# New order of the mixed section of polynomial attention and a gated feed-forward layer, with the last tokens' products written permuted

## The chip, the cores and the metric

The kernel runs on one core of a Trainium2 chip. Its engines are TensorE (PE, with its weight loads as PEld), VectorE (DVE), ScalarE (ACT), GpSimd (POOL) and SyncE (SP, which here only issues transfers). TensorE writes its results to PSUM; GpSimd does not read PSUM in this kernel. The metric is the device time of one launch in microseconds: 286.42 us before the change, the median of three runs (286.40 to 286.61).

## The reference

Attention with a polynomial feature map, then a feed-forward layer with a sigmoid gate, all in float32:

```python
def phi(x):                                   # q, k, v: (4, 4, 1088, 32); S1, S2: (8, 32)
    a = np.einsum('rd,bhsd->bhsr', S1, x)
    b = np.einsum('rd,bhsd->bhsr', S2, x)
    return np.einsum('bhsi,bhsj->bhsij', a, b).reshape(*x.shape[:-1], r * r)
kv = np.einsum('bhsf,bhsd->bhfd', phi(k), v)
z = np.sum(phi(k), axis=2)
attn = np.einsum('bhsf,bhfd->bhsd', phi(q), kv) / (np.einsum('bhsf,bhf->bhs', phi(q), z)[..., None] + 1e-06)
x = attn.transpose(0, 2, 1, 3).reshape(4352, 128)
gate = 1.0 / (1.0 + np.exp(-(x @ w_gate)))    # w_gate, w_val: (128, 1536)
out = (gate * (x @ w_val)) @ w_out            # w_out: (1536, 128)
```

## The kernel before

The 4352 tokens of x lie transposed in SBUF (xT, 128 features by tokens) and are cut into nine chunks: eight of 512 tokens and a last one of 256. The first five chunks are computed in "waves" (w1, line 690), mixed with the attention of the four batches. When the attention is done, at about 177 us, `section()` computes the last four chunks: three of 512 tokens and the last 256.

Within a chunk, the 32 tokens of a partition block are 34 tokens apart in the output, since the attention's tiles take every 34th token of a batch.

**How the section computes gate and value.** For 128 columns of w_gate and the same 128 of w_val, the two products with a chunk form a 2 by 2 problem: gate and value on one side, the two halves of the 128 features between, and two halves of the chunk's tokens on the other. Seven products of half size do the work of eight, with sums of weights (fw) and of tokens (yt) made before. They are P1 to P7 in `feature_of` (line 1561). Each takes 64 rows (the lower or the upper half of the array), 128 columns of weights in two halves of 64, and 256 tokens. One wave w holds two such sets of 128 columns: P1 to P7 for the first, P1' to P7' for the second. Waves 0 to 17 are the three chunks of 512 tokens (six waves each). Waves 18 to 21 are the last 256 tokens; there an entry issues four matmuls over 128 tokens, and the six pairs of column sets are dealt as `ends = ((0, 2), (1, 3), (4,), (5,))`, so that waves 20 and 21 have no primed products.

A wave uses three PSUM banks, A, V and C, and passes through these entries (`gated`, line 1612; ACT entries begin with A or S, DVE entries with D or M):

| entry | engine | what it does | it needs |
|---|---|---|---|
| P1, P2 | PE | add to A | P2 after Aa |
| Aa | ACT | V = A (L1623) | P1 and P1' |
| P6, P7, P4 | PE | add to V | P6 and P7 after Aa; P7 after D1 has read V; P4 after D2 has read V |
| P5, P3 | PE | add to C | P3 after D1 |
| Ac | ACT | s5 = C (L1625) | P5 and P5' |
| D1 | DVE | C = V + s5 (L630) | P6, P6', Ac |
| D2 | DVE | c2 = V + s5 (L630) | P7, P7' |
| Sa, Sc | ACT | sigmoid of A, of C (L1627) | P2; P3 |
| M1, M2 | DVE | g = V times Sa; g = c2 times Sc (L1633, L1635) | P4, Sa; D2, Sc |

A bank is taken again by a later wave once its readers are done. The number behind "=" in an entry names the bank or buffer that it takes.

**The product with w_out** is done in the same way. Q0 to Q3 (`token_sum`, line 1637, POOL) make sums of g over tokens. WLA, WUA, WLB, WUB and WFA, WFB (`w_out`, line 1588) add to two accumulators A and B: L and U name the half of the rows, F all 128 rows at once; the number is the pair of column sets, and -2 and -1 are the two that the waves left over. EA and EB (`empty`, line 1650) copy an accumulator out with ACT and move halves of it across partitions by DMA; chunk numbers go from -1 (the waves' last) to 2. F0 to F6 (`total`, line 1669) add the parts with DVE, transpose (L1683), and store with four or eight transfers on SP (`store`, L550). T0 to T3 (`x_sum`) are POOL's sums of tokens for a chunk.

**The last 256 tokens** end differently (`last`, line 1686). Their g is the stationary operand, in 64 tokens by 128 rows, and w_out's rows stream past it, so the result has tokens on its partitions. O0 and O1 add to the first of two banks (`end`), O2 and O3 to the second. `store_end` (line 560) copies the first bank with ACT and the second with DVE into o_end and stores each with one transfer, the first from ACT's queue and the second from SP's (L566).

**What sets the order.** The four compute engines take their instructions in the order in which the program issues them, and the section issues them in the order of the string `ORDER` (lines 19 to 68): 740 entries, of which 444 are TensorE's. Each engine's order is that of its own entries in it; an engine waits when an operand or a bank is not free. Transfers are issued by SP's queue in the order of their calls, and by ACT's in EA:2, EB:2 and the end.

Of the kernel before, what the change touches and what calls it, by code (L numbers as in the profile page):

```python
# [16 lines left out]
P = 128  # L17

ORDER = """
P5:1=4 P1':0=5 P1:0 P1:1=0 P5':0=1 P1':1 Aa:0=2 WLA:-2.1 WUB:-2.0 Aa:1=3 P5':1 P5:0 P2':0 P6':0 Ac:1=0  # L20
P6':1 P6:0 Ac:0=1 WUB:-1.0 WLA:-1.0 D1:0 P2:1 P6:1 P2':1 P2:0 D1:1 P7':0 P3':0 Sa:0=0 P7:0 P3:0 Sa:1=1
P3':1 P7:1 D2:0=2 Sc:0=3 P1':3=5 P7':1 P5:2=0 P3:1 M2:0=0 P5':2 P4':0 Sc:1=4 D2:1=5 Q0:0 P4:0 P1:2=1
Ac:2=1 WUA:-2.0 P1':2 M1:0 WUB:-1.1 P4:1 Aa:2=4 M2:1=1 P4':1 P1:3 P6:2 P2':2 Aa:3=2 M1:1 Q0:1 P2:2 P6':2
P2':3 P6:3 T0:1 D1:2 P5:3=3 P6':3 T1:1 P5':3 WLB:-2.0 WLA:-1.1 Ac:3=0 Q1:1 P3':2 P2:3 D1:3 P7:2 P3:2 Q1:0
Sa:3=6 WLA:-2.0 P7':2 Sa:2=7 Q2:1 P7':3 P3':3 D2:2=8 Sc:2=2 P3:3 P5':4=5 P1':5=1 P7:3 M2:2=2 Sc:3=3 P4':2
P1':4=0 D2:3=0 P4:2 P1:4 WUA:-1.1 P5:4 Aa:4=3 M1:2 P4':3 P1:5 Ac:4=1 M2:3=3 P4:3 WUA:-1.0 Aa:5=4 WUA:-2.1
P2':4 M1:3 Q0:3 P6:4 P2:4 P6':4 P6:5 Q0:2 Sa:4=4 P5':5=2 WLB:-1.0 D1:4 Q2:0 P6':5 P5:5 P2:5 WLB:-1.1
Ac:5=0 Q1:3 P7:4 P3:4 EA:-1 D1:5 P7':4 P3':4 Q1:2 P1:6=0 P2':5 Sc:4=5 D2:4=1 Q2:2 P1':6 WUA:1.1 Sa:5=2
P3:5 P7:5 T2:1 Aa:6=5 P3':5 P7':5 EB:-1 Q3:2 P5:6=1 WUA:1.0 D2:5=8 P5':6 P4':4 T3:1 P6':6 WLB:1.1 Ac:6=1
Q3:1 P2:6 P4:4 Sc:5=7 P4:5 P6:6 Q3:0 WUA:0.1 P4':5 D1:6 P2':6 WUA:0.0 Q2:3 M1:4=4 WLB:3.1 P1:7=2 Sa:6=0  # L30
Q3:3 WLB:0.0 P1':7 M2:5=5 WUA:2.0 WLB:1.0 Aa:7=3 P5':7=0 WLB:3.0 M2:4 P6':7 P5:7 P3':6 P7:6 M1:5 Ac:7=0
Q0:4 P3:6 P7':6 P2':7 P6:7 Sc:6=3 Q1:4 D2:6=6 WUA:4.1 WLB:2.0 D1:7 Q2:4 P1':8=4 WUA:2.1 P5:8=1 P2:7 F0:-1
WUA:4.0 P1:8 Sa:7=4 F1:-1 P5':8 P3':7 F2:-1 Aa:8=2 P3:7 P7':7 M2:6=6 P7:7 P4':6 Sc:7=7 P2:8 WUB:0.0
D2:7=8 Ac:8=1 Q0:6 P4:6 WLA:3.1 F4:-1 WUB:3.1 WLA:0.1 P1':9=0 P4':7 F3:-1 P6:8 WLA:3.0 M1:6 WLA:0.0 P1:9
P4:7 WUB:1.1 Aa:9=5 Q0:5 WLA:1.0 WUB:2.0 M1:7=0 T0:2 P6':8 P6':9 P6:9 WUB:3.0 D1:8 Q3:4 WLA:2.0 P5':9=3
F5:-1 P5:9 WLA:2.1 Q1:6 WLA:1.1 P2':9 Ac:9=0 P7':8 P2':8 D1:9 Q2:6 P3:8 P7:8 Sa:8=1 WLA:4.0 P2:9 D2:8=5
T1:2 P7:9 WUB:1.0 F6:-1 P3:9 P3':8 Q1:5 P1':10=4 P3':9 Sc:8=2 Q2:5 P7':9 P4':8 Sa:9=3 P4:8 P1:10 Q3:5
D2:9=6 Sc:9=0 P5:10=1 WUB:4.0 Aa:10=0 M2:7 P5':10 WUB:5.1 P1:11=3 P4':9 Ac:10=1 M1:8=2 Q0:7 P2':10 P1':11
M2:8 P4:9 P6':10 Aa:11=2 Q1:7 P2:10 WUA:3.0 M1:9=1 P6:10 P6':11 Sa:10=4 WUA:3.1 WLB:5.1 D1:10 Q3:6
P5':11=5 P6:11 M2:9 WLB:5.0 P5:11 Q2:7 P1':12=4 WUA:5.1 Ac:11=0 P3:10 WUA:5.0 D1:11 P1:12 P7:10 Q0:9  # L40
# [12 lines left out]
WUB:8.0 WLA:10.1 M1:14 WLA:8.0 P6':16 T0:3 P4':15 P6:16 Q1:14 P2:16 P1:17=0 D1:16 WUB:11.1 WLA:9.0 Q0:13
M2:15=2 WLA:9.1 P5':17=3 T1:3 WUB:9.0 P3:16 P3':16 P7:16 M1:15 WLA:10.0 P1':17 Q2:14 Sc:16=6 WLA:11.0
P7':16 Aa:17=2 Q1:13 WLA:11.1 P5:17 D2:16=3 P2':16 WUB:10.0 Ac:17=0 Q2:13 M2:16=1 P2:17 P6:17 EA:1 Q3:12
P6':17 P2':17 Sa:16=7 P1:18=1 P4:16 D1:17 Sa:17=0 P4':16 P1':18 Q3:13 WUB:11.0 WLA:12.0 Aa:18=4 M1:16
P3:17 P5':18=0 EB:1 Q0:16 P6:18 WLA:13.0 F2:1 P6':18 P5:18 Q0:15 P2:18 P3':17 Ac:18=1 WUB:13.1 P7:17
Sc:17=1 D1:18 Q3:14 P7':17 P1:19=5 P1':19 P2':18 F0:1 Q1:15 P7:18 P3':18 Aa:19=3 D2:17=4 P3:18 P7':18
Sa:18=5 F1:1 P6:19 WUA:12.0 Q2:15 Sc:18=8 WUA:12.1 P4:17 D2:18=2 P2':19 P1:20=1 Q1:16 P5:19=0 P4':17
P5':19 WLB:13.0 M1:17=3 T3:3 P2:19 P6':19 Ac:19=0 Q2:16 P4:18 WLB:13.1 Sa:19=3 D1:19 P5:20=2 P4':18 Q3:15  # L60
Aa:20=5 WLB:12.0 WUA:13.1 M1:18=4 Ac:20=1 Q3:16 P7':19 P6:20 P3':19 P7:19 D1:20 P2:20 P3:19 D2:19=6 P7:20
WLA:12.1 Sa:20=7 F3:1 Sc:19=0 WUB:12.0 WLA:13.1 M2:18 P1:21=1 P4:19 P5:21=4 P4':19 F4:1 Aa:21=0 WUB:13.0
P3:20 M2:17 Ac:21=0 P6:21 WUA:13.0 F5:1 WFA:14.0 Q0:17 F6:1 WFA:14.1 D1:21 Q1:17 WFA:15.1 M1:19=6
WFB:16.0 Q2:17 M2:19 WFA:15.0 Q3:17 WFA:16.1 WFA:17.0 D2:20=5 WFA:17.1 WFA:16.0 WFB:17.0 EA:2 WFB:17.1
# [7 lines left out]
def kernel(  # L72
# [17 lines left out]
    NTOK, DM = out.shape  # L90
# [4 lines left out]
    T = S // 32  # L95
# [62 lines left out]
    T0 = 2 * q_chk[0][1]  # L158
# [112 lines left out]
    HALF = TCH // 2  # L271
# [288 lines left out]
    def store_end(acc):  # L560
        b, r = divmod(tok_chk[-1][0], S)
        o_sb = [sbA.tile([P, P], F32, tag="nd", name="o_end") for _ in range(2)]
        for u, copy in enumerate((nc.scalar.copy, nc.vector.tensor_copy)):
            copy(out=o_sb[u], in_=acc[u])
        for u, eng in enumerate((nc.scalar, nc.sync)):
            eng.dma_start(  # L566
                out=bass.AP(
                    tensor=out.tensor,
                    offset=out.offset + (b * S + r // 32 + u) * DM,
                    ap=[[2 * DM, 4], [T * DM, 32], [1, DM]],  # L570
                ),
                in_=o_sb[u],
            )
# [932 lines left out]
    def section():  # L1506
# [41 lines left out]
        def end_g(w):  # L1548
            return gs[home["g", w]].rearrange("p (q u t) -> p q u t", u=2, t=HALF // 2)
# [62 lines left out]
        def gated(k, w):  # L1612
            n = parts_of(w)
            at = lambda x: bank[home[x, w]][:, :n]
            s5, c2 = (lambda: s5s[home["s5", w]][:, :n]), (lambda: smalls[home["c2", w]][:, :n])
            if w < N:
                two = lambda x: x.rearrange("p (j t) -> p j t", j=2)
                g = lambda u: g_of(w)[:, :, u * HALF : (u + 1) * HALF]
            else:
                two = lambda x: x.rearrange("p (q t) -> p q t", t=HALF // 2)  # L1620
                g = lambda u: end_g(w)[:, : 2 * n // HALF, u]
            if k == "Aa":
                nc.scalar.copy(out=at("V"), in_=at("A"))  # L1623
            elif k == "Ac":
                nc.scalar.copy(out=s5(), in_=at("C"))  # L1625
            elif k in ("Sa", "Sc"):
                nc.scalar.activation(out=smalls[home[k, w]][:, :n], in_=at(k[1].upper()), func=ACTF.Sigmoid)  # L1627
            elif k == "D1":
                add(at("C"), at("V"), s5())
            elif k == "D2":  # L1630
                add(c2(), at("V"), s5())
            elif k == "M1":
                nc.vector.tensor_tensor(out=g(0), in0=two(at("V")), in1=two(smalls[home["Sa", w]][:, :n]), op=MUL)  # L1633
            else:
                nc.vector.tensor_tensor(out=g(1), in0=two(c2()), in1=two(smalls[home["Sc", w]][:, :n]), op=MUL)  # L1635
# [135 lines left out]
```

## Time and profile before

| | us |
|---|---|
| median of three runs | 286.42 |
| the profiled execution | 286.56 |
| its span | 284.5 |
| first product of the section | 177.03 |
| first copy of the section's last result (ACT, L564) | 279.66 |
| copies out of the accumulators (ACT, L1659), 128x512, one | 0.58 |
| V and C copies (ACT, L1623 and L1625), 128x512, one | 0.57 |
| sums and gated products (DVE, L630, L1633, L1635), 128x512 / 128x256, one | 0.69 / 0.42 |
| token sums (POOL, L528 and L1648), 128x256, one | 0.72 |

The span is what the profiler sees of the program; the execution's time is 2.06 us longer. "Busy" is the share of the span in which at least one instruction of an engine runs. TensorE runs at its full granted clock throughout (0.997 in the mean). Start times are read from the span's begin.

### The profile page before, as it was taken

To read this page: it belongs to the slowest core of one execution; us is meant where nothing else is said; L and a number is where in the kernel's file an instruction comes from. 1 tells how busy PE (TensorE), PEld (TensorE's weight loads), DVE (VectorE), ACT (ScalarE), POOL (GpSimd) and SP (SyncE) were. 2 spreads that over 40 slices of the span, in tenths; PEclk is the share of its full clock that TensorE was granted. 3 is DMA by queue.
4 is the path that set the end of the run, shared out by engine and by line. 5 is a ranking of instruction groups with operands and counts; after the bars stand their busy time and mean duration, and the time that the engine had idled before them with its cause. 6 is when DMAs were issued, how large, how long until landed. Compare 5 with 4: busy or idle time off the path is not lost.

```text
span 284.5 us, 8360 instructions
## 1 busy us (share of the span) xinstructions
PE 277.5 (98%) x3444; PEld 169.1 (59%) x3444; DVE 207.1 (73%) x349; ACT 123.2 (43%) x242; POOL 177.5 (62%) x238
## 2 busy tenths in 40 slices
PE   8899999999999999999999999999999999999993
PEld 4454433354444444544444544679889889999783
DVE  6987788946778777677769758576777766877861
ACT  3689833222335222533325223566536445465230
POOL 2666673567486578663978764367748784797400
PEclk9999999999999999999999999999999999999998
DMA  7995441674781376554368412100400130121133
GB/s 221 348 365 144 94 158 42 156 135 120 225 184 28 82 168 151 128 158 106 74 159 158 116 27 54 24 2 13 112 3 12 31 85 2 21 45 26 21 68 56
DMA packets 33630, 29.32 MB, mean 103 GB/s; under 512 B 19256, under 2 KB 28024, under 8 KB 33592
## 3 DMA queue, kind: packets, MB, share of 16 engines
q1 hardware_dynamic: 29188, 25.70, 36.5%
q10 hardware_dynamic: 4404, 3.08, 4.2%
q8 instruction: 27, 0.44, 0.7%
q14 instruction: 11, 0.09, 0.1%
HBM read 20.60 MB, written 3.26 MB: 84 GB/s over the span
## 4 chain that ended last, share of the span: by engine, by line
PE 97%; ACT 1%; POOL 0%; DVE 0%; issue 0%
PE wave L690 36%; PE b L538 25%; PE prod L538 23%; PE moeout L582 4%; PE warm L383 2%; PE kvz L1035 1%; PE nps L1393 1%; PE kps L816 1%; PE kvz L1022 1%; PE cqps L962 1%; PE nps L1225 0%; PE denj L1164 0%; PE nps L1177 0%; PE dps L1206 0%; ACT asb L933 0%; POOL gh L850 0%
## 5 line engine op out<-in xcount | busy, mean ns | idle before, releaser
L690 PE MATMUL wave<-xT,w_sb 128*64 128x512 f32 (+2 forms) x436 | 117.4, 589 | 0.1
L538 PE MATMUL prod<-tsum,ws 64*64 64x256 f32 (+1 forms) x348 | 85.7, 379 | 0.0
L538 PE MATMUL b<-yt,fw 64*64 64x256 f32 (+1 forms) x1056 | 77.8, 352 | 0.0
L698 ACT ACTIVATE sg<-wave 128x512 f32<-128x512 f32 x60 | 35.8, 597 | 89.8 <-PE wave L690 85.7
L690 PEld LDWEIGHTS wave<-xT,w_sb 128*64 128x64 f32 (+1 forms) x436 | 40.0, 143 | 46.2 <-issue 35.9
L528 POOL TENSOR_TENSOR tsum<-g,tsum 128x256 f32<-128x256 f32 x48 | 46.2, 963 | 30.3 <-DVE g L725 30.0
L725 DVE TENSOR_TENSOR g<-wave,sg 128x512 f32<-128x512 f32 x60 | 41.1, 685 | 27.3 <-ACT sg L698 26.5
L538 PEld LDWEIGHTS b<-yt,fw 64*64 64x64 f32 x1056 | 54.1, 133 | 7.3 <-issue 1.5
L538 PE MATMUL prod<-g,w_sb 64*64 64x256 f32 (+2 forms) x234 | 56.6, 377 | 0.0
L528 POOL TENSOR_TENSOR tsum<-g 128x256 f32<-128x256 f32 x48 | 41.6, 866 | 16.8 <-DVE g L725 16.5
L538 PEld LDWEIGHTS prod<-tsum,ws 64*64 64x64 f32 (+1 forms) x348 | 43.0, 135 | 9.4 <-issue 6.0
L1648 POOL TENSOR_TENSOR tsum<-g 128x256 f32<-128x256 f32 x36 | 26.9, 760 | 27.1 <-DVE g L1635 21.0
L538 PE MATMUL prod<-tsum,w_sb 64*64 64x256 f32 (+1 forms) x116 | 34.1, 380 | 0.0
L538 PEld LDWEIGHTS prod<-g,w_sb 64*64 64x64 f32 (+1 forms) x234 | 26.4, 135 | 12.6 <-issue 9.3
L538 PE MATMUL prod<-g,ws 64*64 64x256 f32 (+1 forms) x116 | 33.2, 378 | 0.0
L538 PE MATMUL b<-yt,w_sb 64*64 64x256 f32 (+1 forms) x288 | 30.8, 351 | 0.0
L1648 POOL TENSOR_TENSOR tsum<-g,tsum 128x256 f32<-128x256 f32 x36 | 26.9, 760 | 1.2
L1627 ACT ACTIVATE sg<-b 128x512 f32<-128x512 f32 (+1 forms) x34 | 18.9, 580 | 17.0 <-PE b L538 13.8
L630 DVE TENSOR_TENSOR b<-b,s 128x512 f32<-128x512 f32 (+1 forms) x22 | 14.7, 672 | 10.7 <-ACT s L1625 6.7
L538 PEld LDWEIGHTS b<-yt,w_sb 64*64 64x64 f32 x288 | 18.4, 133 | 1.7 <-ACT b L1623 0.2
L538 PEld LDWEIGHTS prod<-g,ws 64*64 64x64 f32 (+1 forms) x116 | 15.5, 135 | 3.8 <-ACT e L1659 0.2
L1625 ACT COPY s<-b 128x512 f32<-128x512 f32 (+1 forms) x22 | 12.3, 570 | 10.7 <-PE b L538 10.6
(162 smaller groups left out, 356.6 us busy)
## 6 DMA issues: line engine op xcount, KB each, us to landing
qp<-dq SPq DMA_DIRECT2D x7, 576.0 KB
bq<-dq SPq DMA_DIRECT2D x14, 288.0 KB
kq<-in_k_dram SPq DMA_DIRECT2D x3, 544.0 KB
kq<-in_q_dram SPq DMA_DIRECT2D x3, 544.0 KB
w_in<-in_moe_w_out_dram SPq DMA_DIRECT2D x6, 256.0 KB
yt<-xT SPq DMA_DIRECT2D x12, 128.0 KB
w_in<-in_moe_w_gate_dram SPq DMA_DIRECT2D x5, 256.0 KB
w_in<-in_moe_w_val_dram SPq DMA_DIRECT2D x5, 256.0 KB
```

The source lines that it names most:

```text
L383: nc.tensor.matmul(out=t[:, 0, :n], lhsT=x, rhs=r, start=True, stop=True)
L528: nc.gpsimd.tensor_tensor(out=t[:, u], in0=in0, in1=in1, op=ALU.subtract)
L538: nc.tensor.matmul(out=out, lhsT=lhsT, rhs=rhs, start=start, stop=stop, skip_group_check=True)
L582: nc.tensor.matmul(out=moe["acc"][d], lhsT=w_sb[:, 2, j, d], rhs=g[:, jj], start=(j == 0), stop=(j == NJ - 1),)
L630: nc.vector.tensor_tensor(out=out, in0=in0, in1=in1, op=ALU.add)
L690: nc.tensor.matmul(out=wv[d, which, jj * tw + o : jj * tw + o + tp], lhsT=w_sb[:, which, j0 + jj, d], rhs=xT[:, t0 + o : t0 + o + tp], sta ...
L698: nc.scalar.activation(out=sg, in_=wv[:, 0], func=ACTF.Sigmoid)
L725: nc.vector.tensor_tensor(out=g, in0=wv[:, 1], in1=sg, op=MUL)
L816: nc.tensor.matmul(out=ts[pi][32 * g : 32 * g + 32, : NJK * 32], lhsT=sk[rows, :], rhs=kT_of[b][rows, KBASE[g] : KBASE[g] + NJK], start=Tr ...
L1625: nc.scalar.copy(out=s5(), in_=at("C"))
L1627: nc.scalar.activation(out=smalls[home[k, w]][:, :n], in_=at(k[1].upper()), func=ACTF.Sigmoid)
L1648: nc.gpsimd.tensor_tensor(out=t[:, out], in0=in0, in1=in1, op=ALU.subtract)
```

## The change

The string ORDER is new: the same 740 entries (the same products, copies, sums and transfers) in another order, with other banks and buffers behind "=". Then two edits for the last 256 tokens. M1 and M2 of waves 18 to 21 write g in another order of tokens: they read their operands as 4 blocks of 32 tokens, as they lie, and write element s of block y to place 4s + y. The result's 128 partitions in o_end then stand in the order 4s + y instead of 32y + s, and the transfers' output pattern has its two outer dimensions exchanged to match. Both transfers still move 128 rows of 512 bytes.

```diff
 ORDER = """
-P5:1=4 P1':0=5 P1:0 P1:1=0 P5':0=1 P1':1 Aa:0=2 WLA:-2.1 WUB:-2.0 Aa:1=3 P5':1 P5:0 P2':0 P6':0 Ac:1=0
-P6':1 P6:0 Ac:0=1 WUB:-1.0 WLA:-1.0 D1:0 P2:1 P6:1 P2':1 P2:0 D1:1 P7':0 P3':0 Sa:0=0 P7:0 P3:0 Sa:1=1
-P3':1 P7:1 D2:0=2 Sc:0=3 P1':3=5 P7':1 P5:2=0 P3:1 M2:0=0 P5':2 P4':0 Sc:1=4 D2:1=5 Q0:0 P4:0 P1:2=1
-Ac:2=1 WUA:-2.0 P1':2 M1:0 WUB:-1.1 P4:1 Aa:2=4 M2:1=1 P4':1 P1:3 P6:2 P2':2 Aa:3=2 M1:1 Q0:1 P2:2 P6':2
-P2':3 P6:3 T0:1 D1:2 P5:3=3 P6':3 T1:1 P5':3 WLB:-2.0 WLA:-1.1 Ac:3=0 Q1:1 P3':2 P2:3 D1:3 P7:2 P3:2 Q1:0
+P1:0=4 WUB:-2.0 P1':1=5 P1':0 P1:1 P5:0=0 Aa:0=1 P5':0 P5':1=2 Aa:1=3 P5:1 WLA:-1.0 Ac:0=0 WLA:-2.1 P6':0
+Ac:1=1 P2':0 P6:0 P6':1 P2:1 D1:0 P6:1 T0:1 P2:0 P2':1 D1:1 P7':0 P3:0 Sa:0=0 P3':0 P7:0 P7':1 P3':1
+Sc:0=1 D2:0=2 P7:1 P3:1 Sa:1=3 WUA:-2.0 P1':2=4 D2:1=4 Sc:1=5 P4':0 P5:2=0 P4:0 P1:2 P1':3=5 P4':1 Aa:2=2
+M1:0=0 WUB:-1.0 P4:1 P5':2 P1:3 M1:1=1 P2:2 P6':2 Aa:3=1 M2:0 WLA:-1.1 P6:2 Ac:2=0 P2':2 P5:3=3 M2:1 Q0:0
+P6':3 P5':3 D1:2 WUB:-1.1 WLA:-2.0 Ac:3=1 P6:3 P2:3 Q1:0 Sa:2=6 P3':2 P7':2 D1:3 Q0:1 P3:2 P7:2 P2':3
...
-WFB:15.0 WFB:15.1 WFB:14.0 Sc:20=2 P7:21 EB:2 M2:20=5 P3:21 P4:20 D2:21=8 P2:21 M1:20 P4:21 F0:2 O3:4=2,3
-F1:2 O0:1 Sc:21=1 O2:4 F2:2 Sa:21=4 O0:2 O1:0 F3:2 O0:0 O1:4 M2:21=1 O3:2 M1:21 O3:0 O2:3 O3:3 F5:2 O1:3
-O1:1 F4:2 O0:4 O3:1 F6:2 O0:5 O1:5 O2:1 O2:5 O1:2 O2:0 O3:5 O0:3 O2:2
+WFB:17.1 WFB:16.0 WFB:17.0 WFB:14.0 P7:21 EB:2 P4:20 P3:21 D2:21=1 M2:20=0 F2:2 P4:21 P2:21 F0:2 O0:1=3,5
+F1:2 Sc:21=4 O3:0 Sa:21=3 O0:3 M2:21=1 O1:3 O2:1 F3:2 O3:1 O1:0 M1:20 O3:2 M1:21 O2:4 O1:2 F5:2 O3:3 O2:5
+F4:2 O2:3 O2:0 F6:2 O2:2 O3:5 O3:4 O0:0 O1:4 O0:5 O0:2 O1:1 O1:5 O0:4
 """
...
@@ store_end
                 out=bass.AP(
                     tensor=out.tensor,
                     offset=out.offset + (b * S + r // 32 + u) * DM,
-                    ap=[[2 * DM, 4], [T * DM, 32], [1, DM]],
+                    ap=[[T * DM, 32], [2 * DM, 4], [1, DM]],
                 ),
...
@@ gated, for waves 18 to 21
-                two = lambda x: x.rearrange("p (q t) -> p q t", t=HALF // 2)
-                g = lambda u: end_g(w)[:, : 2 * n // HALF, u]
+                two = lambda x: x.rearrange("p (q y s) -> p q y s", y=4, s=32)
+                g = lambda u: end_g(w)[:, : 2 * n // HALF, u].rearrange("p q (s y) -> p q y s", y=4)
```

Some steps of the new order that the prediction speaks of, counted along TensorE's entries from 0 (an entry on all 128 rows counts two): P7:21 stands at step 429 in both lists; P4:21 at 433 before and 432 after; EA:0 at 229 and 227, EB:0 at 227 and 225, F2:0 at 277 and 265, F6:-1 at 175 and 237, F6:0 at 311 and 329, F6:2 at 449 and 448; P4:1 at 37 and 36, P3':2 at 51 in both.

## The prediction

> **What bounds the kernel now.** I read the page first, then the chain of waits from 160 us on, then the timeline of the weight loads from 177 us (what an instruction stood idle for, in brackets), then the engines' busy time in four short stretches at the end. From the page, sections 1 and 4:
>
> ```profile
> PE 277.5 (98%) x3444; PEld 169.1 (59%) x3444; DVE 207.1 (73%) x349; ACT 123.2 (43%) x242; POOL 177.5 (62%) x238
> PE 97%; ACT 1%; POOL 0%; DVE 0%; issue 0%
> ```
>
> TensorE sets the end and hardly rests, so a new order can win only what TensorE loses between products. 98% busy hides that, since overlapping products count as busy. So I go by starts. From the chain of waits (start, us, what):
>
> ```profile
> 180.32 0.42 PE prod L538 x2
> 180.75 0.44 PE prod L538 x3
> ...
> 181.41 3.67 PE b L538 x68
> ```
>
> One entry of ORDER issues two matmuls, one per column half, recorded as four MATMULs: 68 records are 17 entries in 3.67 us, 0.216 us each. I call this a step. The list holds 406 P and W entries of one step, 14 WF entries on all 128 rows (two steps) and 24 O entries (one): 458 steps, 98.9 us. The section's first product starts at 177.03 and the first copy of its last result at 279.66: 102.6 us. So 3.7 us are lost. That is all the order can touch, and part of it is no wait: the entries of the last 256 tokens issue twice as many, half as long matmuls. Where the large losses are, in the timeline of the weight loads:
>
> ```profile
> 180.75 0.13 PEld L538 LDWEIGHTS prod<-tsum,w_sb 64*64 64x64 f32 x1 [0.46 <-POOL tsum L528]
> 186.46 0.64 PEld L538 LDWEIGHTS b<-yt,fw 64*64 64x64 f32 x16 [0.33 <-ACT b L1623]
> 203.79 1.27 PEld L538 LDWEIGHTS b<-yt,fw 64*64 64x64 f32 x26 [0.26 <-ACT b L1623]
> 223.79 0.25 PEld L538 LDWEIGHTS b<-yt,fw 64*64 64x64 f32 x8 [0.18 <-DVE b L630]
> 254.29 0.19 PEld L538 LDWEIGHTS b<-yt,fw 64*64 64x64 f32 x3 [0.31 <-issue]
> ```
>
> Lost against the step: 0.39 us at WUB:-1.0, 0.25 at P6:2, 0.10 at P6':7, 0.09 at P7':11, 0.37 at P6:18, and about 0.05 more at the next entry each time. L1623 is Aa, the copy that V needs before P6 and P7 add to it. P6:18 names no releaser, but its copy ran from 253.60 to 254.17, so it is the same wait.
>
> The end: first the queues in the timeline, then the engines' busy time by stretch, whose last two numbers are DMA share and GB/s:
>
> ```profile
> 278.14 1.95 SPq L550 DMA_DIRECT2D out_dram<-o_sb  x4
> 279.96 1.13 ACTq L566 DMA_DIRECT2D out_dram<-o_end  x1
> 280.54 0.65 SPq L566 DMA_DIRECT2D out_dram<-o_end  x1
> ```
>
> ```profile
> 278.14:278.97 0.83, 0.83 (x20) 0.83 (x18) 0.00 (x0) 0.00 (x0) 0.00 (x0) 1.00 0.00 0
> ...
> 279.90:281.24 1.34, 0.00 (x0) 0.00 (x0) 0.28 (x1) 0.03 (x1) 0.00 (x0) 1.00 0.80 118
> 281.24:282.14 0.90, 0.00 (x0) 0.00 (x0) 0.00 (x0) 0.00 (x0) 0.00 (x0) 1.00 0.27 71
> 282.14:283.04 0.90, 0.00 (x0) 0.00 (x0) 0.00 (x0) 0.00 (x0) 0.00 (x0) 0.70 0.26 75
> ```
>
> The last two transfers move 64 KB each in 0.90 us (71 GB/s by 0.90 us is 64 KB), one after the other, on a quarter of the 16 DMA engines: 4. Just before, the o_sb stores kept 80% busy. What differs is the output pattern: o_sb's begins with 32 rows, o_end's with 4.
>
> **The order.** The same 444 TensorE entries stand in the list, so the 98.9 us stay. What moves is the lead, the steps between an entry and the one that needs its result by way of another engine. For Aa: P1':2 starts at 185.13 and P6:2 could start at 186.46, 1.33 us or 6.2 steps from start to start. That is a lead of 5.2, and 4 was given. Before, waves 2, 7 and 18 have a lead of 4 and five others 5; after, no wave has less than 6 but wave 20 (5) and wave 21 (4). Gone: 0.25 + 0.10 + 0.37 + 3 x 0.05 = 0.87 us. WUB:-1.0 waited for the last of Pool's three token sums (end 180.70). It moves from step 14 to step 35: 0.44 us gone. Sum: 1.31 us.
>
> Against it stand new waits. WLA:-1.0 moves from step 15 to step 9, 177.03 + 9 x 0.216 = 178.97; its sum is Pool's instruction at 179.29 less 0.02, ready 179.32, and products follow Pool by 0.05 (180.70 to 180.75): a wait of 0.40 us. D1:2 now stands on VectorE behind M1:1, M2:0 and M2:1. M1:1 waits for P4:1, step 36, which is read 0.43 to 0.65 us after its start, by the section's copies; with 0.65, at step 39. Four instructions of 0.69 us, D1:2 the last (2.76 us, 12.8 steps), and 0.1 us of hand-over then hold P3':2 until step 52.3; it stands at 51: 0.27 us. Both waits are TensorE's own, so all entries behind them shift. Near the end the lead from P7:21 to P4:21 falls from 3 to 2 steps, and Aa's for wave 21 from 5 to 4: up to 0.22 us each. I take 0.2 for both, since the first has 0.33 us of waiting there today and another instruction may cover it. Sum: 0.87 us.
>
> The smaller losses (0.14 at P7':11, 0.12 at P7':3, 0.12 at P2:15, 0.06 each at P7:12 and P4:16, 0.1 at P2:18) come to 0.6 us. Their neighbours are all different after. I take 0.4 as gone. The list: -1.31 + 0.87 - 0.4 = **-0.8 us**. Bounds: -1.9 if none of the new waits comes; +0.5 if the new ones double and the small ones stay.
>
> On SP's queue the eight stores of F6:-1 (4.65 us of issue at 216.80) move behind the copies of EA:0 and EB:0 and the load of the last tokens, and that load (2.4 us) between two copies. Nothing: the first to read these copies, F2:0, is 38 steps or 8 us behind EA:0, and one after the other they take 1.2 + 0.5 + 2.4 + 0.6 us to issue. A store has no reader but the transpose that reuses its buffer, 92 steps on. Were that cover gone, up to the load's 2.4 us would come out.
>
> **The end's transfers.** The order of dimensions is turned, 32 rows first, like o_sb's. The trace has no o_end transfer in this form, so I bound it: unchanged 0.90 us, or, over 16 engines, a quarter of that, 0.23 us. I take the second, by the o_sb row. Today SP's, issued at 280.54, only begins at 282.14 when ACT's has left the same four engines. Spread out, ACT's ends at 281.24 + 0.23 = 281.47 and SP's can begin once issued, some 0.83 us (o_sb's: issued at 278.14, no data before 278.97) to 1.28 us (ACT's: 279.96 to 281.24) after 280.54: 281.4 to 281.8. It ends at 281.6 to 282.05 instead of 283.04, 1.0 to 1.4 us earlier; 0 if nothing spreads. SP cannot be earlier than its four o_sb stores, which follow the transpose of F6:2. F6:2 stands one step earlier, but M2:20 has moved behind D2:21, which waits for P7:21, and may push it back by 0.3. I take **-1.0 us**.
>
> **The permuted products.** M1 and M2 of waves 18 to 21 write each element 16 bytes from the last one. No row has such a write. Nearest on one side: 0.69 us for g in runs, taken unchanged, 0. On the other: two reductions of the same 128 numbers (L1118), 272 ns in runs and 371 ns at steps of 32 bytes, 0.77 ns an element, so 0.20 us per 256 elements. Four such products stand in VectorE's last chain, which runs without rest from 272.80 to 278.11 into F6:2: 0 to 0.8 us, which would hold up SP's stores. I take 0: the slow row is a strided read by another operation, and the write leaves the order of reads as it is. The Trainium skill, page "SBUF — State Buffer", section "Door 1: The DMA port swizzle (why `[64,N]` ≈ `[32,N]`)", speaks against me: it says accesses that go to a new 16-byte line each time pay a penalty, for 4-byte numbers at just this step. The L1118 pair agrees in kind, no write here does; by it the end would be as in the rival on writes below.
>
> The sum: -0.8 - 1.0 = -1.8. The profiled execution took 286.56 us (span 284.5 and 2.06 around it), so 284.76; it lies 0.14 above the median, so **284.6 us** for the median.
>
> **Rivals.**
> - The new waits eat what the old ones gave, and only the transfers gain: 286.42 - 1.0 = 285.4. For it: the new waits above are nearly as long as the old ones. Against: 0.4 us of small losses.
> - The list gives nearly all it can and the transfers too: -1.9 - 1.3, 283.2. For it: the leads are more even (the smallest for Aa rises from 4 to 6 for 20 waves).
> - The transfers don't gain, because they spread no wider or SP's are held by the o_sb stores: 285.6. Against: the 0.80 row.
> - Writes at 16 bytes cost twice: 0.27 us per 256 elements (0.69 - 0.42, the row of 256, is what 256 elements take), four in the last chain, +1.1, which undoes the transfers' gain: 285.7.
> - Slower: they cost three times. +0.54 four times, 2.2 us, into F6:2 and SP's last stores; and +1.07 for each of the four products of 512 at about 260 to 266 us, where VectorE is 67% busy (17.38 of 26 us from 254 on), which makes D1 and D2 of waves 20 and 21 late: about 1 us more. 286.42 - 1.8 + 3.2 = 287.8. It decides from about 2.4 times on. For it: only the reduction pair, which is at 1.7 times per element at most (0.77 beside 1.05 ns); against: no row shows three times.
>
> **Chances.** Forecast (284.0 to 285.2) 0.48; only the transfers 0.16; everything 0.14; no gain at the end 0.09; writes twice 0.07; slower 0.06. About 0.2%, 0.57 us, is what a measurement can tell from no change: 285.85 and 286.99 are the borders. Of the middle cases some 0.07 ends within them. So faster 0.87, same 0.07, slower 0.06. The range of 8 in 10 goes from 283.2 to 285.7.
>
> **What would show it.** Right: the copy of the last result starts about 0.8 us earlier; no waits behind L1623 at waves 2, 7 and 18; a Pool wait near 179.3 at WLA:-1.0 and one behind a VectorE L630 near 188.4; the last two transfers at a DMA share well above 0.27 and overlapping o_sb's. Wrong: L1633 and L1635 of the last waves over 0.69 and 0.42 us, the last transfers still at 0.27, or new TensorE waits of over 0.5 us in the middle.

## The result, and the profile after

| | before | after |
|---|---|---|
| median of 20 runs each, us | 286.49 | 285.99 |
| ratio, with its 95% interval | | 0.9982 (0.9975 to 0.9989) |
| the profiled execution / its span, us | 286.56 / 284.48 | 285.86 / 284.06 |

The change is faster by 0.50 us, where 1.8 us were forecast, and 285.99 lies outside the range of 283.2 to 285.7. A few executions ran at a lower granted clock and take no part in the times here; the only profiled one of e1_list is among them (clock 0.754, 364.47 us), so its stages are not read. The same page lines as before, sections 1 and 4, of the changed kernel:

```profile
PE 276.2 (97%) x3444; PEld 160.2 (56%) x3444; DVE 208.6 (73%) x349; ACT 123.3 (43%) x242; POOL 182.3 (64%) x238
PE 95%; DVE 1%; ACT 1%; DMA 1%; issue 0%; POOL 0%; SPq 0%; DVEq 0%
```

TensorE is still busy nearly throughout, with 1.3 us less of it: the loss between products in the section fell from 3.75 to 3.01 us (from the start of its first product to that of its last, 102.41 and 101.68 us, less 457 steps of 0.2159). The timeline of the weight loads, in four short windows of the changed kernel, shows which waits are left (in brackets):

```profile
179.16 0.13 PEld L538 LDWEIGHTS prod<-tsum,ws 64*64 64x64 f32 x1 [0.25 <-POOL tsum L528]
...
186.57 0.97 PEld L538 LDWEIGHTS b<-yt,fw 64*64 64x64 f32 x16
...
253.81 1.23 PEld L538 LDWEIGHTS b<-yt,fw 64*64 64x64 f32 x38
...
272.79 0.14 PEld L538 LDWEIGHTS b<-yt,fw 64*64 64x64 f32 x2 [0.31 <-DVE sg L630]
```

The waits for Aa (L1623) near 186.5 and 254 are gone. One at WLA:-1.0 has come (0.19 us against the step), and one at P4:21, which waits for D2:21 (0.45 against the step). But TensorE does not decide the end. The timeline of the last 7 us, all engines and queues:

```profile
277.49 0.71 DVE L1683 STREAM_TRANSPOSE o_sb<-y 128x512 f32<-128x512 f32 x1
278.12 0.25 DVE L564 COPY o_end<-b 128x128 f32<-128x128 f32 x1
278.23 2.09 SPq L550 DMA_DIRECT2D out_dram<-o_sb  x4
278.92 0.27 ACT L564 COPY o_end<-b 128x128 f32<-128x128 f32 x1 [4.05 <-PE b L538]
279.21 0.63 ACTq L566 DMA_DIRECT2D out_dram<-o_end  x1
280.43 0.65 SPq L566 DMA_DIRECT2D out_dram<-o_end  x1
```

Read it from the bottom. SP's o_end is issued last, at 280.43, against 280.54 before. Its data had been ready since 278.37, when VectorE's copy ended. It stood on SP's queue behind the four o_sb stores, and these follow F6:2's transpose, which ends at 278.20 (before: 278.11). TensorE's last product starts 0.73 us earlier after the section's first; ACT copies its result at 278.92, and nothing that comes last waits for it. (Before the change the last product, O2:2, went to the second bank, which VectorE copies at 279.88; ACT's copy at 279.66 was of the first bank.)

The engines' busy time by stretch (last two columns: DMA share, GB/s) for the changed kernel:

```profile
279.21:280.73 1.52, 0.00 (x0) 0.00 (x0) 0.00 (x0) 0.00 (x0) 0.00 (x0) 1.00 0.79 114
280.73:281.72 0.99, 0.00 (x0) 0.00 (x0) 0.00 (x0) 0.00 (x0) 0.00 (x0) 1.00 0.76 150
281.72:282.08 0.36, 0.00 (x0) 0.00 (x0) 0.00 (x0) 0.00 (x0) 0.00 (x0) 1.00 0.65 182
282.08:282.54 0.46, 0.00 (x0) 0.00 (x0) 0.00 (x0) 0.00 (x0) 0.00 (x0) 1.00 0.00 0
```

ACT's o_end moves among the o_sb data in the second stretch, SP's fills the third: 64 KB in 0.36 us at a share of 0.65, where it took 0.90 at 0.26 before. The transfers do spread.

The last piece is behind the transfers. The lines of the kernel's closing code on Pool's queue, before and after the change (columns: count, ns min/median/max, first and last start in us):

```profile
L1766 POOLq DRAIN  x2: 39/58/78, 284.0 to 284.2; - x2
L1766 POOLq EVENT_SEMAPHORE_RANGE_CLEAR  x1: 96/96/96, 284.1 to 284.1; - x1
```

```profile
L1766 POOLq DRAIN  x2: 77/132/187, 283.1 to 283.6; - x2
L1766 POOLq EVENT_SEMAPHORE_RANGE_CLEAR  x1: 96/96/96, 283.2 to 283.2; - x1
```

Pool's last DRAIN followed RANGE_CLEAR's start by 0.13 us and took 39 ns; now it follows by 0.42 and takes 187 ns. From the last transfer's report to the span's end it was 1.11 us; now it is 1.54.

### The profile page after: what moved, and what is told of

It is laid out like the page before. It is cut to its first block, busy times and chain, and to the rows that moved or that the text cites. A ratio compares the mean times of both kernels' runs of the same rounds, so it can differ in the third digit from the quotient of the medians.

```text
span 284.1 us, 8365 instructions
## 1 busy us (share of the span) xinstructions
PE 276.2 (97%) x3444; PEld 160.2 (56%) x3444; DVE 208.6 (73%) x349; ACT 123.3 (43%) x242; POOL 182.3 (64%) x238
## 4 chain that ended last, share of the span: by engine, by line
PE 95%; DVE 1%; ACT 1%; DMA 1%; issue 0%; POOL 0%; SPq 0%; DVEq 0%
PE wave L690 36%; PE b L538 25%; PE prod L538 23%; PE moeout L582 4%; PE kvz L1035 1%; PE nps L1393 1%; PE kps L816 1%; DMA s_in<-in_S_dram 1%; PE kvz L1022 1%; PE cqps L962 1%; PE nps L1225 0%; PE denj L1164 0%; PE nps L1177 0%; PE dps L1206 0%; ACT asb L933 0%
## 5 line engine op out<-in xcount | busy, mean ns | idle before, releaser
L538 PE MATMUL prod<-tsum,ws 64*64 64x256 f32 (+1 forms) x348 | 87.1, 379 | 0.0
L538 PE MATMUL b<-yt,fw 64*64 64x256 f32 (+1 forms) x1056 | 80.3, 351 | 0.1
L528 POOL TENSOR_TENSOR tsum<-g,tsum 128x256 f32<-128x256 f32 x48 | 46.2, 963 | 30.4 <-DVE g L725 30.0
L538 PE MATMUL prod<-g,w_sb 64*64 64x256 f32 (+2 forms) x234 | 53.6, 377 | 0.0
L528 POOL TENSOR_TENSOR tsum<-g 128x256 f32<-128x256 f32 x48 | 41.5, 865 | 16.8 <-DVE g L725 16.5
L1648 POOL TENSOR_TENSOR tsum<-g 128x256 f32<-128x256 f32 x36 | 28.0, 793 | 22.4 <-DVE g L1635 18.6
L538 PEld LDWEIGHTS prod<-g,w_sb 64*64 64x64 f32 (+1 forms) x234 | 25.4, 135 | 13.6 <-issue 9.1
L1648 POOL TENSOR_TENSOR tsum<-g,tsum 128x256 f32<-128x256 f32 x36 | 29.8, 844 | 0.5
L1627 ACT ACTIVATE sg<-b 128x512 f32<-128x512 f32 (+1 forms) x29 | 15.8, 569 | 15.1 <-PE b L538 13.0
L538 PEld LDWEIGHTS b<-yt,w_sb 64*64 64x64 f32 x288 | 17.3, 133 | 2.7 <-issue 0.8
L1623 ACT COPY b<-b 128x512 f32<-128x512 f32 (+1 forms) x22 | 12.2, 559 | 13.7 <-PE b L538 11.1
L630 DVE TENSOR_TENSOR sg<-b,s 128x512 f32<-128x512 f32 (+1 forms) x17 | 11.2, 658 | 9.2 <-PE b L538 9.0
```

Source lines behind the costliest of these rows:

```text
L528: nc.gpsimd.tensor_tensor(out=t[:, u], in0=in0, in1=in1, op=ALU.subtract)
L538: nc.tensor.matmul(out=out, lhsT=lhsT, rhs=rhs, start=start, stop=stop, skip_group_check=True)
L630: nc.vector.tensor_tensor(out=out, in0=in0, in1=in1, op=ALU.add)
L1648: nc.gpsimd.tensor_tensor(out=t[:, out], in0=in0, in1=in1, op=ALU.subtract)
```

## The ledger

Runs differ by up to 0.6 us in when the section starts (one by 3 us), well ahead of the change, so all profiles are set against their own first product of the section. A time is then the sum of: where F6:2's transpose ends, from there to the report of the last transfer, from there to the span's end ("closing"), and what the time has beyond its span ("outside"). The last two columns set that sum and the median against the kernel before, the median against that of its own series.

| kernel | last TensorE product | F6:2 ends | to the report | closing | outside | sum | sum less before | median less before |
|---|---|---|---|---|---|---|---|---|
| before | 102.41 | 101.08 | 5.26 | 1.11 | 2.08 | 109.53 | | |
| after | 101.68 | 101.40 | 4.32 | 1.54 | 1.80 | 109.06 | -0.47 | -0.50 |
| e2_end | 102.51 | 101.42 | 4.42 | 1.11 | 2.09 | 109.04 | -0.49 | -0.49 |
| e3_spread | 101.69 | 100.91 | 4.31 | 1.53 | 1.89 | 108.64 | -0.89 | -0.85 |
| e4_writes | 101.67 | 101.37 | 4.97 | 1.54 | 1.89 | 109.77 | +0.24 | +0.28 |
| e5_pool | 101.74 | 101.44 | 4.28 | 1.10 | 1.79 | 108.61 | -0.92 | -0.82 |
| e6_sp | 101.68 | 101.39 | 4.07 | 1.54 | 1.90 | 108.90 | -0.63 | -0.89 |
| e7_f6 | 101.75 | 100.90 | 4.31 | 1.54 | 1.91 | 108.66 | -0.87 | -1.08 |
| e8_reads | 101.68 | 101.48 | 4.23 | 1.54 | 1.79 | 109.04 | -0.49 | -0.51 |
| e9_all | 101.82 | 100.50 | 4.32 | 1.10 | 1.79 | 107.71 | -1.82 | -1.79 |
| e10_before_pool | 102.64 | 101.32 | 5.15 | 1.55 | 1.80 | 109.82 | +0.29 | +0.34 |
| e11_idle | 102.34 | 101.38 | 4.27 | 1.54 | 1.88 | 109.07 | -0.46 | -0.60 |
| e12_list_pool | 101.72 | 100.94 | 5.57 | 1.10 | 1.79 | 109.40 | -0.13 | -0.11 |

The change, by this ledger: F6:2 0.32 us later, the transfers 0.94 shorter, the closing 0.43 longer, the part outside the span 0.28 shorter. TensorE's last product is 0.73 earlier and stands in no term.

## The experiments

**The two parts apart, and the two end edits apart.** e1_list is the new ORDER alone:

```diff
-                    ap=[[T * DM, 32], [2 * DM, 4], [1, DM]],
+                    ap=[[2 * DM, 4], [T * DM, 32], [1, DM]],
...
-                two = lambda x: x.rearrange("p (q y s) -> p q y s", y=4, s=32)
-                g = lambda u: end_g(w)[:, : 2 * n // HALF, u].rearrange("p q (s y) -> p q y s", y=4)
+                two = lambda x: x.rearrange("p (q t) -> p q t", t=HALF // 2)
+                g = lambda u: end_g(w)[:, : 2 * n // HALF, u]
```

> The new ORDER alone: the last 256 tokens' products and the two last transfers as before the change. Theory (the end is no longer set by TensorE but by VectorE's chain into F6:2, then SP's four o_sb stores and the o_end transfer behind them on that queue): the products of 256 cost 0.42 us again, F6:2's transpose ends near 277.5 us instead of 278.20, SP's o_end is issued near 279.8, and its data wait for ACT's transfer on the same four DMA engines (280.5 to 281.4), ending near 282.3 and reported near 282.65, against 282.52 in the changed kernel: 286.1 us. Rival (TensorE sets the end and the two end edits give the forecast 1.0 us): 287.0, the changed kernel and 1.0. The prediction's own term for the list would give 285.6.

Measured: 287.01 us against 286.54 before, ratio 1.0020 (1.0007 to 1.0033): the new ORDER alone makes the kernel slower. That is 0.9 us above what my theory gave, so a cost was missing from it. e12_list_pool below has the same ORDER and a trace that can be read.

e2_end is the kernel before with the two edits of the end (the same lines, the other way).

> Both end edits on the old ORDER. Theory (the permuted write costs 0.22 us a product of 256, four of them in a chain without rest into F6:2): the transpose ends near 279.0 instead of 278.11, SP's o_end is issued near 281.2 and is reported near 283.3, as before the change (283.37): 286.4 us. Rival (the transfers give 1.0 us by themselves, as forecast): 285.5.

Measured: 286.05 against 286.54, ratio 0.9988 (0.9978 to 0.9997). So the end edits alone give all that the whole change gives, and both numbers of mine were off. F6:2 ended only 0.34 later in the ledger, not 0.9: VectorE's instructions overlap, and a permuted product of 256 lasts 0.64 us but lets the next one start 0.46 after it where the plain one did so after 0.34; two of the four stood ahead of short waits that took it.

e3_spread takes the permuted writes out of the changed kernel, e4_writes its new transfer pattern (the first or the second half of the diff above alone); in both the last 256 tokens' rows come out in another order.

> The changed kernel with g written in runs as before, the transfers in the new pattern: the last 256 tokens' rows come out in another order. Theory (the permuted writes hold up F6:2 and with it SP's queue): L1633 and L1635 of 256 back at 0.42 us, F6:2's transpose ends about 0.65 us earlier (the first of the four hides in a wait for Sc:21), the last transfer is reported near 281.9, 285.35 us. Rival (TensorE and ACT's transfer set the end): 286.0, no change beyond 0.2.

> The changed kernel with the transfers' old pattern (4 rows first): the last 256 tokens' rows come out in another order. Theory (SP's o_end cannot begin before o_sb's data end at 281.7, and spreading shortens it from 0.90 to about 0.35): 0.55 us more, 286.5 us. Rival (spreading is worth the forecast 1.0 us): 287.0.

Measured: e3 285.69, ratio 0.9970 (0.9958 to 0.9982); e4 286.82, 1.0005 (0.9989 to 1.0021). Without the permuted writes F6:2 ends 0.49 earlier (100.91 instead of 101.40), and the time is 0.30 lower than the changed kernel's. Without the spread transfers the stretch from F6:2 to the report is 0.65 longer and the time 0.83 higher. Both times lie between their two expectations. Each permuted product, lines for L1633 from 255 us (e3) and 270 us (after) on; columns: ns min/median/max:

```profile
L1633 DVE TENSOR_TENSOR g<-b,sg x3: 415/426/683, 259.1 to 276.3; 128x256 f32<-128x256 f32 x2, 128x512 f32<-128x512 f32 x1
```

```profile
L1633 DVE TENSOR_TENSOR g<-b,sg x2: 631/640/648, 275.8 to 276.2; 128x256 f32<-128x256 f32 x2
```

Two products of 256 at 0.42 us in e3 (its third is one of 512), at 0.64 in the changed kernel.

**Reading permuted instead of writing permuted.** e8_reads:

```diff
-                two = lambda x: x.rearrange("p (q y s) -> p q y s", y=4, s=32)
-                g = lambda u: end_g(w)[:, : 2 * n // HALF, u].rearrange("p q (s y) -> p q y s", y=4)
+                two = lambda x: x.rearrange("p (q y s) -> p q s y", y=4, s=32)
+                g = lambda u: end_g(w)[:, : 2 * n // HALF, u].rearrange("p q (s y) -> p q s y", y=4)
```

> The changed kernel with the same permuted g made the other way: elements of g written one after the other, the operands read 128 bytes apart (V in PSUM, Sa, Sc and c2 in SBUF). If the writes at 16 bytes are what costs (0.64 us for 256 elements against 0.42), the products are back at 0.42 us and the time is that of the kernel with g in runs, 285.69 in the same series as 285.99 for the changed one: 285.7. If any permuted access costs it, 0.64 again or more, and 286.0 or more.

Measured: 286.05 us, 0.9985 (0.9977 to 0.9994): no gain.

```profile
L1633 DVE TENSOR_TENSOR g<-b,sg x3: 586/596/671, 259.6 to 276.8; 128x256 f32<-128x256 f32 x2, 128x512 f32<-128x512 f32 x1
L1633 DVE TENSOR_TENSOR g<-b,c x2: 1024/1043/1062, 267.1 to 268.4; 128x512 f32<-128x512 f32 x2
```

Operands 128 bytes apart cost nearly as much (0.59 us) as results 16 bytes apart. So it is not the write as such. The Trainium skill, page "SBUF — State Buffer", section "Door 1: The DMA port swizzle (why `[64,N]` ≈ `[32,N]`)", says that each access that goes to a new 16-byte line pays a penalty. Both forms do so at each element in SBUF (one operand of e8_reads lies in PSUM), and the measured price is a factor of 1.4 to 1.5 for 256 elements; no run separates this cause from others.

**Pool's closing.** In the new ORDER Pool's trace has 327 instructions instead of 323: four more waits for semaphores (the expectations below count one more in each case, and so 326th and 209th for what is the 325th and the 208th here). The trace also records transfers of instructions, 8 KB each: in the kernel before, one starts when SP has begun its 81st and one when it has begun its 209th instruction, 128 apart, and another when Pool has begun its 196th. Just ahead of its two transfers SP pauses, for 0.44 us ahead of its 80th instruction and for 0.38 us ahead of its 208th (280.09 to 280.47 before the change), between issues that else stand 0.05 apart. All 13 traces read here have both pauses, whatever SP's 208th instruction is. The next border for Pool would come 128 instructions after its 196th, at about its 324th; the 325th is the slow DRAIN. e5_pool puts instructions ahead of it:

```diff
+            if item == "F3:1":
+                pad = sbA.tile([P, 1], F32, tag="pad", name="pad", bufs=1)
+                for _ in range(14):
+                    nc.gpsimd.memset(pad, 0.0)
```

> The changed kernel with 14 tiny Pool memsets of a tile that nobody reads, where Pool is idle at F3:1. Theory (an engine pauses about 0.4 us where its instructions go over into a next block of 128; with the new ORDER Pool has 4 instructions more, and the border falls into the closing sequence, ahead of its 326th instruction, the last DRAIN: 0.41 us from RANGE_CLEAR's start to that DRAIN's against 0.13 before the change): the border now falls on the last memset, at about 262 us, where Pool waits anyway; the stretch from the last transfer's report to the end of the span falls from 1.54 to 1.11 us, and the time to 285.57 us. Rival (the DRAIN is slow for a reason that the order of products brings, such as later work on Pool): the stretch stays at 1.54 and the time at 286.0.

Measured: 285.74 us, 0.9983 (0.9966 to 0.9999): the median lies between the two expectations, the closing is 1.10 us, as the theory has it. Its closing lines, then those of e10_before_pool, which has the same lines with `range(4)` in the kernel before the change:

```profile
L1770 POOLq EVENT_SEMAPHORE_RANGE_CLEAR  x1: 96/96/96, 283.5 to 283.5; - x1
L1770 POOLq DRAIN  x1: 39/39/39, 283.6 to 283.6; - x1
```

```profile
L1770 POOLq DRAIN  x2: 78/130/183, 284.0 to 284.6; - x2
...
L1770 POOLq EVENT_SEMAPHORE_RANGE_CLEAR  x1: 96/96/96, 284.1 to 284.1; - x1
```

> The kernel before the change with 4 tiny Pool memsets at F3:1, so that Pool has as many instructions as in the changed kernel, and nothing else. Theory (the border of Pool's block of 128 instructions now falls ahead of the last DRAIN): the stretch from the last transfer's report to the end of the span rises from 1.11 to 1.53 us, 0.42 us more, 286.95 us. Rival (the DRAIN depends on the order of the section): nothing, 286.5.

Measured: 286.89 against 286.55, 1.0013 (0.9999 to 1.0027). The slow DRAIN goes with 14 instructions and comes with 4, whatever the order of products: it hangs on the count. (The time of e10_before_pool alone, whose interval reaches 0.9999, would not decide it; the closing lines do.) The ledger adds what neither theory had: with 323 instructions the time outside the span is 2.08 or 2.09 us, with the border elsewhere 1.79 to 1.91. The kernel before also has a transfer of instructions at 285.90 us, 1.42 behind its span's end; the changed kernel, whose border lies in the closing, has it at 284.36, 0.30 behind; e5_pool, e9_all and e12_list_pool have none there. So the border seems to have been paid for before the change too, for the most part behind the span's end; no instruction is recorded there, so this is inferred from the count. Moving it into the closing costs 0.43 - 0.28 = 0.15 us net, by the profiles; taking it out of the end altogether, as e12_list_pool does below, gains the 0.29 outside as well. The Trainium skill, page "Runtime: NRT & Kernel Launch", section "Instruction fetch mechanics", has blocks of 256 instructions and a border that is mostly hidden; here SP's borders lie 128 apart, Pool's fit the same length, and a border costs 0.38 to 0.43 us where the engine has nothing to wait for.

**SP's border.** In the changed kernel it lies ahead of the fourth o_sb store (SP's queue, the first three stores and the fourth):

```profile
278.23 1.40 SPq L550 DMA_DIRECT2D out_dram<-o_sb  x3
280.00 0.32 SPq L550 DMA_DIRECT2D out_dram<-o_sb  x1
```

e6_sp cuts the eight stores of F6:-1 into sixteen, so that the border falls on an earlier store (its pause, 0.37 us, now ends at 269.89):

```diff
+                for h in ((0, n),) if ci != SECT - 1 else ((0, n // 2), (n // 2, n)):
-                eng.dma_start(
...
-                        ap=[[T * DM, 32], [DM, n], [1, 32]],
+                            ap=[[T * DM, 32], [DM, h[1] - h[0]], [1, 32]],
```

> The changed kernel with the eight stores of F6:-1 cut into sixteen of half the tokens, so that SP has eight instructions more ahead of the end. Theory (SP's own border of a block lies ahead of its 209th instruction, which is the fourth o_sb store of F6:2 in the changed kernel, where 0.38 us pass between two issues that else stand 0.05 apart): the four stores are issued without that pause, o_end is issued 0.33 us earlier, and the last transfer is reported as much earlier: 285.65 us. Rival (the 16 DMA engines, at 0.8 to 0.95 of their time in o_sb's data, set the end, not the issues): 285.95 to 286.0.

```profile
278.62 1.95 SPq L551 DMA_DIRECT2D out_dram<-o_sb  x4
280.67 0.64 SPq L567 DMA_DIRECT2D out_dram<-o_end  x1
```

Measured: 285.67 us, 0.9972 (0.9961 to 0.9982), 0.32 below the changed kernel. The four stores now take 1.95 us of queue instead of 2.09; the fourth, which began 1.80 us after the transpose, begins 1.47 after it, its data end 0.30 sooner (3.25 instead of 3.55), and the report comes 0.25 sooner. o_end's issue itself moved by 0.15 only, not by the 0.33 that I gave, since the fourth store now takes about 0.5 us to issue like the two before it, and took 0.32 after the pause. In both kernels o_end's data begin 1.29 us after that issue, so 0.15 of the 0.25 is the issue; the rest is the report, which follows the end of the data by 0.35 us here and by 0.44 in the changed kernel. The time of 285.65 was met, but not by the step that I gave for it.

**Which chain sets the end.** e7_f6 changes the changed kernel's ORDER:

```diff
-O2:1 F3:2 O3:1 O1:0 M1:20 O3:2 M1:21 O2:4 O1:2 F5:2 O3:3 O2:5
-F4:2 O2:3 O2:0 F6:2 O2:2 O3:5 O3:4 O0:0 O1:4 O0:5 O0:2 O1:1 O1:5 O0:4
+O2:1 F3:2 O3:1 O1:0 M1:20 O3:2 F5:2 O2:4 O1:2 F4:2 O3:3 O2:5
+F6:2 M1:21 O2:3 O2:0 O2:2 O3:5 O3:4 O0:0 O1:1 O0:2 O0:4 O1:4 O0:5 O1:5
```

> The changed kernel with F5:2, F4:2 and F6:2 ahead of M1:21 on VectorE, and the products that need M1:21 (O0:5, O1:5, O0:4, O1:4) last. Theory (VectorE's chain into F6:2 starts what sets the end): the transpose ends 0.45 to 0.5 us earlier after the section's start (at 101.4 now), all of SP's issues with it, and TensorE's last product no more than 0.15 us later; the time falls by 0.4 to 285.6. Rival (TensorE's last result and ACT's transfer behind it set the end): 286.0 or up to 0.15 more.

Measured: 285.48 us, 0.9966 (0.9941 to 0.9991), 0.5 below the changed kernel; F6:2 ends 0.50 earlier in the ledger, TensorE's last product 0.07 later.

e11_idle goes at it from the other side: it makes TensorE late and leaves VectorE alone.

```diff
+            if item == "O0:4":
+                idle = bank[4][:, :DM]
+                for x in range(6):
+                    product(idle[half_of(x % 2)], end_g(N)[:, 0, 0][:, half_of(x % 2)], w_sb[:, 2, 0, :], True, True)
```

> The changed kernel with three more entries' worth of products (six of 64x128, into a bank that nobody reads any more) ahead of O0:4, the last entry: TensorE ends 0.65 us later, where it ended before the change. Theory (TensorE's end is not on the path, so that the 0.73 us won there are worth nothing): up to 0.1 us, 286.0 to 286.1. Rival (TensorE's last result and ACT's transfer set the end, as the forecast's sum has it): 0.65 us, 286.65.

```profile
278.78 2.09 SPq L550 DMA_DIRECT2D out_dram<-o_sb  x4
280.14 0.27 ACT L564 COPY o_end<-b 128x128 f32<-128x128 f32 x1 [4.70 <-PE b L538]
280.44 0.64 ACTq L566 DMA_DIRECT2D out_dram<-o_end  x1
280.98 0.64 SPq L566 DMA_DIRECT2D out_dram<-o_end  x1
```

Measured: 285.95 us, 0.9981 (0.9972 to 0.9989). TensorE ends 0.66 us later (102.34), ACT's copy starts 1.36 us after SP's first issue instead of 0.69, and the time is that of the changed kernel (285.99). This is the direct answer for the changed kernel: what the list wins at TensorE's end is worth nothing there.

e12_list_pool is e1_list with the 14 memsets of e5_pool.

> The new ORDER alone (products and transfers at the end as before the change) with Pool's 14 memsets, which take the border of its block out of the closing sequence. Theory (TensorE's 0.73 us end ahead of a chain that they do not shorten, and the new ORDER alone was slower than the kernel before by 0.47 only for Pool's border): TensorE's last product starts 0.7 us earlier after the section's start than before the change (102.4), the last transfer is reported within 0.15 us of where it was (106.3 after the section's start), and the time is 286.5 to 286.6, that of the kernel before. Rival (the list is worth 0.8 by itself, as the prediction's sum has it, and something else in the new ORDER costs as much): 285.75.

Measured: 286.36 against 286.47, 0.9990 (0.9973 to 1.0006): no difference. Stretches as above:

```profile
279.22:281.45 2.23, 0.30 (x6) 0.06 (x2) 0.00 (x0) 0.27 (x1) 0.00 (x0) 1.00 0.76 114
281.45:282.14 0.69, 0.00 (x0) 0.00 (x0) 0.00 (x0) 0.00 (x0) 0.00 (x0) 1.00 0.37 50
282.14:282.83 0.69, 0.00 (x0) 0.00 (x0) 0.00 (x0) 0.00 (x0) 0.00 (x0) 1.00 0.29 82
282.83:283.59 0.76, 0.00 (x0) 0.00 (x0) 0.00 (x0) 0.00 (x0) 0.00 (x0) 1.00 0.24 73
```

TensorE is 0.69 us earlier than before the change, and ACT's transfer is issued 0.48 us earlier after the section's first product. But its data begin 3.10 us after F6:2's transpose, as before the change (3.13), and the four DMA engines that they use still carry o_sb: the share drops to 0.37 from 281.45 on, while o_sb's data last until 282.14. These end 3.79 us after the transpose, against 3.12 before the change and 3.46 in e3_spread, which has the same ORDER and products but spread transfers. So about 0.33 of the delay goes with the new ORDER itself (SP's border, above) and 0.33 with the old transfer pattern, whose data now overlap o_sb's on four engines. F6:2 is 0.14 earlier, the stretch to the report 0.31 longer, and the 0.29 outside the span make up for it. Since the new ORDER brings these costs along, this run alone would leave room for a gain at TensorE that they eat up; e11_idle shows none in the changed kernel.

**All together.** e9_all has the edits of e5, e6 and e7, and M1:20 behind F6:2 too:

```diff
-O2:1 F3:2 O3:1 O1:0 M1:20 O3:2 M1:21 O2:4 O1:2 F5:2 O3:3 O2:5
-F4:2 O2:3 O2:0 F6:2 O2:2 O3:5 O3:4 O0:0 O1:4 O0:5 O0:2 O1:1 O1:5 O0:4
+O2:1 F3:2 O3:1 O1:0 O3:2 F5:2 O2:4 O1:2 F4:2 O3:3 O2:5
+F6:2 O2:3 M1:20 O2:0 O2:2 M1:21 O3:5 O3:4 O0:0 O1:1 O0:2 O0:4 O1:4 O0:5 O1:5
```

> The three cures together (Pool's 14 memsets, the sixteen half stores of F6:-1, F5:2, F4:2 and F6:2 ahead of M1:21) with M1:20 behind F6:2 as well. If they are costs of one chain, one behind the other, they add up: against the changed kernel -0.4 (Pool's border), -0.33 (SP's border), -0.5 (F6:2 ahead of M1:21) and up to -0.4 more for M1:20, 284.4 us; TensorE's last product within 0.2 us of where it was. Rival (ACT's transfer behind TensorE's last product takes over as the end once SP's is earlier): 284.9 to 285.1.

```profile
277.18 0.71 DVE L1684 STREAM_TRANSPOSE o_sb<-y 128x512 f32<-128x512 f32 x1
277.82 1.07 DVE L1634 TENSOR_TENSOR g<-b,sg 128x256 f32<-128x256 f32 x2
277.92 1.95 SPq L551 DMA_DIRECT2D out_dram<-o_sb  x4
278.74 0.28 DVE L565 COPY o_end<-b 128x128 f32<-128x128 f32 x1
279.65 0.27 ACT L565 COPY o_end<-b 128x128 f32<-128x128 f32 x1 [4.13 <-PE b L538]
279.94 0.63 ACTq L567 DMA_DIRECT2D out_dram<-o_end  x1
279.97 0.65 SPq L567 DMA_DIRECT2D out_dram<-o_end  x1
```

Measured: 284.76 us against 286.55, ratio 0.9936 (0.9923 to 0.9949): 1.79 us faster than the kernel before and 1.2 faster than the changed one. It lies between the two expectations: F6:2 is 0.90 earlier than in the changed kernel, but the two o_end transfers are now issued within 0.03 us of each other, so TensorE's last result and SP's queue end together (SP's data begin 1.53 us after their issue there, against 1.29 in the changed kernel). That the next gain has to shorten both is what I expect from this; no run tests it.

## Why the prediction was wrong

The step that failed is the sum, "-0.8 - 1.0 = -1.8".

- **The list, -0.8.** Right where it was worked out: TensorE's last product starts 0.73 us earlier after the section's first. Of its terms, the waits for Aa went as forecast; WLA:-1.0 cost 0.19 instead of 0.40, the wait behind D1:2 0.04 instead of 0.27, and the one at the end more (0.45 at P4:21 alone, on D2:21, where 0.2 stood for it and Aa:21 together). (The 102.6 us of the prediction end at ACT's copy of the first bank, 279.66, and not at the last result's, 279.88; this changes the loss by 0.2 us and not the gain.) It isn't part of the time: e11_idle gives 0.66 of it back at no cost, and e12_list_pool, with the list alone, is no faster. The first paragraph said that TensorE "sets the end". The chain of waits of the kernel before ends so (start, us, what):

```profile
279.86 0.02 issue
279.88 0.29 DVE o_end L564
```

It stops at the last copy, 280.17, and the span at 284.48; of the transfers between it says nothing. By the packets of that trace, o_sb's data end at 281.23, ACT's o_end moves from 281.24 to 282.20 and SP's from 282.12 to 283.04, without a gap. ACT's data begin 1.28 us after their issue, as soon as in any run here, so TensorE's end and the stores met at that point, and an earlier TensorE alone found the engines taken (e12_list_pool). No run makes TensorE late in the kernel before, so whether its end held anything up there is not shown. The term on the transfers, for its part, took SP's issue as standing at 280.54. Before the change that issue came behind VectorE's copy (280.17), but also behind the four stores, which are done at 280.09 and follow F6:2's transpose, and SP's pause (to 280.47). With the new list VectorE's copy is done at 278.37; the stores and the pause alone hold the issue, and it moved by 0.11. So a gain at TensorE and a gain worked out from that issue could not be added.
- **The transfers, -1.0.** Right in size: 0.94 less from F6:2's end to the report, 64 KB in 0.36 us at a DMA share of 0.65. Step by step after F6:2's end: SP's issue comes 0.20 sooner, its data begin 0.29 sooner after it, since they no longer wait for ACT's, they take 0.36 us instead of 0.92, and the report follows 0.11 later. The prediction had 0.23 for the data, and 0.83 to 1.28 from issue to data, where 1.29 was measured.
- **The permuted products, taken as 0 of 0 to 0.8.** Wrong within its bounds: 0.64 us instead of 0.42, 0.49 on F6:2's end (after against e3_spread), 0.30 in the time. By the row of 0.42 this is 1.5 times, between "unchanged" and the rival of twice (which put 0.27 on each of four, where 0.22 was measured and only about 0.12 passed on to the next instruction); that rival's 285.7 was the nearest to the result, for part of its reasons.
- **F6:2.** "May push it back by 0.3": it came 0.32 later, but that is luck: by the list it came 0.17 sooner (e3_spread against before), and the writes, for which the prediction took nothing, put 0.49 on it.
- **SP's queue.** It was costed at the eight stores of F6:-1, of which the ledger shows no cost. What the prediction didn't see was the border of SP's instructions among the last stores (by e6_sp 0.25 us to the report, of which 0.15 is o_end's issue, and 0.32 in the time; before the change it lay between the stores and o_end) and Pool's, moved into the closing (0.15 net by the profiles). Neither has an entry in ORDER or a line in the diff.

So the change's sum by the ledger is F6:2 +0.32, transfers -0.94, Pool's border +0.15: -0.47, and -0.50 was measured; the -0.8 of the list is in none of its terms. Up to 0.26 us of difference between ledger and medians (e6, e7) is taken as the scatter of single profiled executions and was not followed further.

## What to carry to other kernels

Follow the end from the last transfer's report back through its queue, not from the last instruction of the busiest engine: a chain that ends at a copy says nothing of the stores behind it. Before two gains are added, ask of each whether it still counts when the other is had; making a busy engine end late on purpose (six idle products here) answers in one run whether its end is on the path. In the last microseconds, count instructions per queue too, since an edit that adds four waits to an idle engine can move a pause to where everyone waits for it.

## What the runs showed of the hardware that I had not expected

An engine's queue paused 0.38 to 0.43 us where it went from one block of 128 instructions to the next (SP ahead of its 208th, Pool ahead of its 325th), and the pause moved with the count of instructions alone (e5_pool, e6_sp, e10_before_pool). A part of the time outside the profile's span, 0.28 us of 2.08, goes when Pool has four instructions more and nothing else is changed (e10_before_pool, 1.80), so it is probably such a pause too. And a VectorE product whose 4-byte operands lie 128 bytes apart lasts about as long (0.59 us for 256) as one whose results lie 16 bytes apart (0.64), against 0.42 in runs.
